# Charging a planner for VectorE's wait on GpSimd, moving weight sums between engines, and re-dividing PSUM banks

## Chip, cores and metric

The kernel runs on one core of one Trainium2 chip. The metric is device time in microseconds of one execution. The time before is 971.36 us, the median of three runs (970.76 to 972.66).

## What is computed

The reference chains three layers; every matrix product is done in float32 there, while the kernel uses pairs of float16 halves (a high and a low part) and three products in place of one.

```python
# attention: q, k, v are (4, 8, 576, 64), f is (4, 8, 576)
decay = cum[:, :, :, None] - cum[:, :, None, :]          # cum = cumsum(log f)
attn = softmax(where(causal, -1e9, q @ k.T / 8 + decay))
x = attn @ v                                             # -> 2304 tokens x 512
# first MLP: 512 -> 2048 -> 512
x = relu(x @ w_in) ** 2 @ w_out
# second MLP: 512 -> 1536 -> 512
out = (silu(x @ w_gate) * (x @ w_val)) @ w_out2
```

## The kernel before

**The order.** The kernel doesn't leave the order of its instructions to a scheduler. Each piece of work is a `Step` with an engine, an estimated duration, what it waits for, the buffers that it takes, and a priority; `Plan.order` plays the steps through in a model of the five engines and emits them in the order in which they started there. Each engine then runs its own list strictly in that order. The model has a rule for VectorE and GpSimd working at once: a step whose function name is in `SHARED` (for VectorE `lo`, `join`, `a2`, `v_lo`, `p_lo`; for GpSimd all its large ones) is lengthened by 0.95 (VectorE) or 0.45 (GpSimd) of its overlap with such a step of the other engine, and never by more than that share of its own duration. Priorities are numbers written out by hand: `EPRI` for the 16 first-half attention units, `VPRI` for the four batches of v, `IPRI`, `ILOAD`, `OPRI`, `OLOAD` for the first MLP's weights and their loads, `GPRI` for the second MLP's weights. A lower number goes first; evictions and the like have -100 to -120.

**The stages.** TensorE begins with 130 matmuls on constants (L295), the lowest priority of all, which the plan puts wherever TensorE would have nothing to do. First come the weights of the first MLP and the first 256 queries of each attention unit (half 0), then the first MLP's tiles `mlp1(j)`, interleaved with the other queries (half 1, tiles of up to 128 queries against up to 576 keys). `mlp1` goes over nine tiles of 256 tokens in the order 0, 1, 2, 3, 4, 5, 6, 8, 7. A tile is eight pairs: 24 matmuls up (L1152), relu and square on ScalarE (the square of the last two tiles on VectorE, `a2`, L1179), the high half on ScalarE (L1195), the low half on GpSimd (`g_lo`, L1198), and 24 matmuls down (L1220) into two PSUM accumulators, which are evicted to `tmp` buffers at the tile's end, one by ScalarE (L1239) and one by VectorE (L1241), and stored.

When attention has ended, its SBUF and PSUM are given to the second MLP. Its gate and value weights, in three chunks `u` each, need for each of the six chunks four sums of 128x512 elements, after Strassen and Winograd (`split7`: `tt`/`sum_of`, L507, all on GpSimd), before ScalarE and VectorE (L545) split seven blocks into halves. `tables2` (L1642 to L1649) works out three-column tables of scales on VectorE. `mlp2` then runs five rounds over two token tiles (one for the tail): the input's maximum (L1286, L1290), a matmul that spreads it over partitions (L1294), `scales` (L1298 to L1302, where L1300 and L1301 multiply three columns by one), four differences on GpSimd (L1317), seven splits (L1354 on ScalarE, `lo` L1358 on VectorE), and then six pairs of seven products (L1415), whose sums VectorE makes (L1432), silu and multiplication (L1456, L1460, L1464 `mul3`), and matmuls L1531 into four accumulators. Chunk `u` of the weights serves pairs 2u and 2u+1.

**PSUM.** Of eight banks `ps_acc` has 3 (accumulators of `mlp1`, and in the early stage the statistics of the first MLP's weights), `ps_h` 2, and `ps_at` (attention: scores take two, the product with v one) 3. In the second MLP `ps_at` becomes two `ps_v` banks and one `ps_l`, the fourth accumulator.

Of the kernel before, what the change touches and what calls it, by code (L numbers as in the profile page):

```python
# [57 lines left out]
class Plan:  # L58
# [9 lines left out]
    def add(self, eng, us, fn, deps=(), pri=0, take=(), use=(), nbytes=0, order=(), late=0.0):  # L68
        deps, order = ([d for d in ds if d is not None] for ds in (deps, order))
        st = Step(len(self.steps), eng, us, fn, deps, order, pri, take, nbytes)  # L70
        st.hot = getattr(fn, "__name__", "") in SHARED[eng] if eng in SHARED else False
        st.late = late
        for buf in (*take, *use):
            buf.users.append(st)
        self.steps.append(st)
        return st

    def order(self):
        now, dma_free = 0.0, 0.0
        free = {e: 0.0 for e in AFTER}  # L80
        hot = {DVE: 0.0, POOL: 0.0}
        landed = []
# [101 lines left out]
def decay_attention_moe_kernel(ctx: ExitStack, tc, q, k, v, f, w1, w2, wg, wv, wo, outT):  # L184
# [19 lines left out]
    HN = 2  # L204
    AN = 3
    XN = 2
# [11 lines left out]
    dpool = ctx.enter_context(tc.tile_pool(name="dram", bufs=1, space=bass.MemoryType.DRAM))  # L218
    ps_acc = ctx.enter_context(tc.tile_pool(name="ps_acc", bufs=3, space=bass.MemoryType.PSUM))
    ps_h = ctx.enter_context(tc.tile_pool(name="ps_h", bufs=HN, space=bass.MemoryType.PSUM))  # L220
# [92 lines left out]
    def bank(where):  # L313
        if where == "acc":
            return Buf("acc", 3), lambda: ps_acc.tile([P, 512], F32, tag="acc", name="ps")
# [169 lines left out]
    def split7(c, idx, slot, scaled):  # L485
# [18 lines left out]

        def tt(out, x, y, op):
# [8 lines left out]
        t2 = add(POOL, 0.3 + pool_us(512), tt(s2, s1, e0, ALU.subtract), [t1], pri, use=[r0])  # L514
        t3 = add(POOL, 0.3 + pool_us(512), tt(s3, e0, o0, ALU.subtract), [j0, j1], pri, use=[r0, r1])
        t4 = add(POOL, 0.3 + pool_us(512), tt(s4, e1, s2, ALU.subtract), [t2], pri, use=[r0, r1])

# [161 lines left out]
    def attn_unit(idx, b, pr, half, opened):  # L679
# [88 lines left out]
        for ti, i in enumerate(tiles):  # L768
# [14 lines left out]
            for h, r0, r1, qc, M, g in heads:  # L783
# [349 lines left out]
    def mlp_pair(t, j, p, np_, names, lag, xs, xbuf, xdeps):  # L1133
# [59 lines left out]
        def g_hi():  # L1193
            G[k0].append(mlp.tile([P, 2, 2, TN], F16, tag="g", bufs=GN, name="g"))
            nc.scalar.copy(G[k0][1][:, 0], G[k0][0])  # L1195

        def g_lo():
            nc.gpsimd.tensor_tensor(G[k0][1][:, 1], G[k0][0], G[k0][1][:, 0], op=ALU.subtract)  # L1198

        h = add(ACT, act_us(512) - 0.07, g_hi, [r], -100, take=[gb], use=[tmp])  # L1200
        l = add(POOL, pool_us(512), g_lo, [h], -100, use=[tmp, gb])
        nm = names[-1]
        if p == 0:
            A[t, j] = [None, None]
            ABUF[t, j] = [Buf("acc", 3), Buf("acc", 3)]
            STORED[t, j] = []
# [55 lines left out]
    def mlp2(n, js, gate):  # L1262
# [106 lines left out]
        if two:  # L1369
            accs = [Buf("acc", 3) for _ in range(3)] + [Buf("al", 1)]  # L1370
        else:
            accs = [Buf("acc", 3) for _ in range(2)]
        STORED[key] = []
# [5 lines left out]
        def acc_new(i):  # L1379
            shape = [P, 512] if two else [P, 2, TN]  # L1380
            if i == 3:
                acc[i] = pools["psl"].tile(shape, F32, tag="al", name="acc")
# [239 lines left out]
    def open_ex():  # L1622
# [5 lines left out]
        pools["psl"] = ctx.enter_context(  # L1628
            tc.tile_pool(name="ps_l", bufs=1, space=bass.MemoryType.PSUM, reuse_waits="tile")
        )  # L1630
# [90 lines left out]
```

## Time and profile before

| | |
|---|---|
| median of three runs | 971.36 us |
| the profiled execution's own time | 972.56 us |
| its span, first to last instruction | 970.9 us |
| TensorE matmul busy | 952.9 us, 98% of the span |
| VectorE, ScalarE, GpSimd busy | 629.4, 607.2, 352.3 us |

An engine's busy time is the union of its instructions' times. A wait of TensorE shows as idle time before an instruction, with the instruction on another engine that released it. The time outside the span (1.7 us) lies before the first and after the last instruction.

### The profile page before, as it was taken

The numbers are of one execution on the slowest core, as the hardware profiler recorded it, in microseconds if no ns is written. First come the engines' busy times: TensorE is split into PE (matmuls) and PEld (weight loads), VectorE is DVE, ScalarE is ACT, GpSimd is POOL, SyncE is SP. The second block draws the span as 40 slices with busy tenths as digits, with TensorE's granted clock in tenths as the row PEclk, the third lists the DMA queues.
The fourth block names the chain that finished last, engine by engine and source line by source line (L and its number), as shares of the span: only waits on it lengthen the run. The fifth ranks groups of instructions, "written<-read, shape, count | busy, mean of one in ns | idle before, by whom it ended". The sixth has DMA issues, their size and how long they took to land. (4 is left out here: it accounts for less than half of the span.)

```text
span 970.9 us, 22565 instructions
## 1 busy us (share of the span) xinstructions
PE 952.9 (98%) x8941; PEld 735.6 (76%) x8941; DVE 629.4 (65%) x1394; ACT 607.2 (63%) x1145; POOL 352.3 (36%) x440
## 2 busy tenths in 40 slices
PE   8999999999999999999999998999999999999998
PEld 3677777888777778777788887777978776877774
DVE  5778878576666687878799999345464363433341
ACT  5889898788777889867787766325443343332232
POOL 1322154354444544533285874122231231110120
PEclk8999999999999999999999999999999999999999
DMA  8697529676777879898943602002001001000101
GB/s 282 209 349 213 105 65 210 180 219 141 168 154 172 174 171 256 181 270 200 248 159 101 226 22 66 1 1 64 26 21 46 1 1 45 1 1 12 34 1 44
DMA packets 147945, 117.47 MB, mean 121 GB/s; under 512 B 98240, under 2 KB 136128, under 8 KB 142592
## 3 DMA queue, kind: packets, MB, share of 16 engines
q1 hardware_dynamic: 147840, 116.04, 45.8%
q8 instruction: 70, 1.15, 0.5%
q14 instruction: 35, 0.29, 0.1%
HBM read 83.44 MB, written 9.51 MB: 96 GB/s over the span
## 5 line engine op out<-in xcount | busy, mean ns | idle before, releaser
L1152 PE MATMUL h<-x,i 128*128 128x256 f16 x1728 | 210.5, 274 | 0.7 <-ACT hold L1174 0.7
L1220 PE MATMUL acc<-g,o 128*128 128x256 f16 x1728 | 208.0, 273 | 1.8 <-POOL g L1198 1.8
L1152 PEld LDWEIGHTS <-i 128*128 128x128 f16 x1728 | 163.1, 98 | 30.7 <-issue 9.6
L1220 PEld LDWEIGHTS <-o 128*128 128x128 f16 x1728 | 163.1, 98 | 29.6 <-issue 8.5
L1531 PE MATMUL acc<-o,f 128*128 128x512 f16 (+1 forms) x720 | 145.7, 358 | 0.5 <-ACT o L1504 0.5
L1531 PEld LDWEIGHTS <-f 128*128 128x128 f16 x720 | 69.9, 98 | 64.5 <-issue 0.8
L1198 POOL TENSOR_TENSOR g<-tmp,g 128x512 f16<-128x512 f32 x56 | 77.1, 1378 | 102.4 <-ACT g L1195 95.3
L1494 POOL TENSOR_TENSOR tmp<-tmp,o 128x256 f32<-128x256 f32 (+1 forms) x30 | 23.5, 784 | 246.9 <-ACT o L1488 246.9
L787 POOL TENSOR_SCALAR_AFFINE_SELECT bias<-bias 128x128 f32<-128x128 f32 (+1 forms) x160 | 68.0, 433 | 122.3 <-DVE cg L826 68.8
L846 ACT ACTIVATE s<-s,cg 128x256 f32<-128x256 f32 (+4 forms) x144 | 83.6, 582 | 21.4 <-DVE cg L826 21.0
L826 DVE CUSTOM_DVE_ANT_0 s<-ps,bias 128x512 f32<-128x512 f32 (+3 forms) x160 | 73.1, 481 | 32.6 <-PE ps L803 28.0
L909 DVE SCALAR_TENSOR_TENSOR p<-s,cg,p 128x512 f16<-128x512 f32 (+4 forms) x112 | 77.9, 710 | 25.2 <-ACT p L905 24.5
L905 ACT ACTIVATE p<-s,cg 128x512 f16<-128x512 f32 (+4 forms) x112 | 67.6, 619 | 13.0 <-DVE cg L859 4.0
L1415 PEld LDWEIGHTS <-g 128*128 128x128 f16 x720 | 65.4, 98 | 10.6 <-issue 2.7
L1460 ACT ACTIVATE r<-r,ms 128x768 f32<-128x768 f32 (+1 forms) x30 | 26.2, 872 | 73.9 <-DVE r L1432 73.7
L1415 PEld LDWEIGHTS <-v 128*128 128x128 f16 x720 | 65.4, 98 | 6.5
L1415 PE MATMUL v<-i,g 128*128 128x256 f16 (+1 forms) x540 | 67.9, 262 | 1.8 <-DVE r L1432 1.6
L1415 PE MATMUL v<-i,v 128*128 128x256 f16 (+1 forms) x540 | 67.9, 262 | 0.0
L1432 DVE TENSOR_TENSOR r<-r,h 128x512 f32<-128x512 f32 (+1 forms) x30 | 19.0, 633 | 72.6 <-PE h L1415 64.0
L1498 POOL TENSOR_TENSOR r<-r,o 128x768 f32<-128x768 f32 (+1 forms) x30 | 44.9, 1498 | 42.5 <-ACT o L1491 41.7
L1432 DVE TENSOR_TENSOR r<-r,v 128x512 f32<-128x512 f32 (+1 forms) x60 | 38.0, 633 | 34.1 <-PE v L1415 32.0
L1415 PEld LDWEIGHTS <-eg 128*128 128x128 f16 x540 | 49.3, 98 | 11.3 <-issue 2.5
(184 smaller groups left out, 1648.7 us busy)
## 6 DMA issues: line engine op xcount, KB each, us to landing
raw<-in_moe_w_out_dram SPq DMA_DIRECT2D x11, 1024.0 KB, 7.7
bias<-cum_d SPq DMA_DIRECT2D x16, 576.0 KB, 4.3
raw<-in_moe_w_val_dram SPq DMA_DIRECT2D x9, 1024.0 KB, 5.5
raw<-in_moe_w_gate_dram SPq DMA_DIRECT2D x9, 1024.0 KB, 7.0
raw<-in_moe_w_in_dram SPq DMA_DIRECT2D x8, 1024.0 KB, 6.7
vr<-in_v_dram SPq DMA_DIRECT2D x32, 256.0 KB, 4.1
x_d<-tmp SPq DMA_DIRECT2D x18, 256.0 KB, 2.8
kr<-in_k_dram SPq DMA_DIRECT2D x16, 288.0 KB, 4.1
```

The costliest lines, as they stand in the source:

```text
L787: nc.gpsimd.affine_select(diag, diag, pattern=[[-1, w]], compare_op=ALU.is_ge, fill=-8e9, base=0, channel_multiplier=1)
L826: nc.vector.tensor_tensor_reduce(out=s[r0:r1, n0:e1], in0=c["ps", ti, ci, h][r0:r1, : e1 - n0], in1=c["bias"][r0:r1, h, n0:e1], scale=-0.1 ...
L846: nc.scalar.activation(s[:, :ext], s[:, :ext], AF.Exp, bias=cg[:, mc : mc + 1], scale=-1.0, accum_out=cg[:, 2:3],)
L905: nc.scalar.activation(pv[:, 0, :ext], s[:, :ext], AF.Copy, scale=cg[:, 3:4])
L909: nc.vector.scalar_tensor_tensor(pv[:, 1, :ext], s[:, :ext], cg[:, 3:4], pv[:, 0, :ext], op0=ALU.mult, op1=ALU.subtract,)
L1152: nc.tensor.matmul(HP[key][:, u, :], w[:, wi, kk, c * P : (c + 1) * P], x[:, xi, kk, :], start=(kk == 0 and (wi, xi) == (0, 0)), stop=(kk ...
L1198: nc.gpsimd.tensor_tensor(G[k0][1][:, 1], G[k0][0], G[k0][1][:, 0], op=ALU.subtract)
L1220: nc.tensor.matmul(acc[:, d - part[0], :], w[:, wi, c, d * P : (d + 1) * P], G[k0][1][:, gi, u, :], start=(m == 0 and d == part[0] and (wi ...
L1415: nc.tensor.matmul(R[reg][:, which, :w], t[:, wh, w1_ : w1_ + P], x[:, xh, xi, kk], start=fresh and which == 0 and kk == 0 and (wh, xh) == ...
L1432: nc.vector.tensor_tensor(out(), x(), y(), op=ALU.add)
L1498: nc.gpsimd.tensor_tensor(g, g, R["g"][:, 0, 1:4], op=ALU.subtract)
L1531: nc.tensor.matmul(acc_of(d), wd[:, cc, d * P : (d + 1) * P], R["g"][:, gi, 2 * m : 2 * m + 2].rearrange("p a t -> p (a t)"), start=mm == ...
```

## The change

It alters five things. (1) The planner's rule for VectorE and GpSimd: every GpSimd step, and on VectorE the steps named in a shorter list with `mul3`, `g_lo` and `sum_of` added, now start late, by all (VectorE) or 0.45 (GpSimd) of what the other engine's step still has to run. (2) Three of the four sums of each weight chunk go to VectorE (`SUMV = 3`; the list `on` sends `t1`, `t2` and `t3` to VectorE and leaves `t4` on GpSimd). (3) `tables2` and `scales` multiply column by column, with a column as the scalar. (4) `ps_acc` gets two banks and `ps_at` four; the second MLP's accumulators are two of `ps_acc` and two of `ps_l`. (5) The hand-written priorities have other values. `GLO = 9` lets tiles from j = 9 on make the low half on VectorE; j ends at 8, so no tile does. The number of matmuls on constants stays 130.

```diff
+PORT = {DVE: 1.0, POOL: 0.45}
+GLO = 9
+SUMV = 3
-SHARED = {
-    DVE: ("lo", "join", "a2", "v_lo", "p_lo"),
-    POOL: ("sum_of", "diff_of", "g_lo", "gd1", "gd3", "k_lo", "q_lo", "mask"),
-}
-SLOW = {DVE: 0.95, POOL: 0.45}
+SHARED = ("lo", "join", "a2", "v_lo", "p_lo", "mul3", "g_lo", "sum_of")
...
-        st.hot = getattr(fn, "__name__", "") in SHARED[eng] if eng in SHARED else False
+        st.hot = eng == POOL or (eng == DVE and getattr(fn, "__name__", "") in SHARED)
...
-                    us = st.us
+                    begin = now
                     if st.hot:
-                        other = hot[POOL if e == DVE else DVE] - now
-                        us += SLOW[e] * max(0.0, min(us, other))
-                        hot[e] = now + us
-                    free[e] = now + us
-                    st.done = now + us + AFTER[e]
+                        begin += PORT[e] * max(0.0, port[POOL if e == DVE else DVE] - now)
+                        port[e] = begin + st.us
+                    free[e] = begin + st.us
+                    st.done = free[e] + AFTER[e]
...
-GPRI = 895
+GPRI = 863
...
-EPRI = [84, -11, -1228, -173, 17, 207, 26, -63, 272, 261, 415, 539, 152, 235, -12, -45]
-VPRI = [11, -292, 536, 601]
-IPRI, ILOAD = [303, -473, 276, 202], [-471, 170, 327, -259]
-OPRI, OLOAD = [279, 410, 340, 342], [-413, 225, 178, 605]
+EPRI = [97, 98, -1473, -437, 74, 58, -88, -342, 192, 243, 591, 593, 223, 341, 56, -118]
+VPRI = [79, -116, 547, 595]
+IPRI, ILOAD = [573, -458, 265, 171], [-574, -104, -303, 434]
+OPRI, OLOAD = [157, 400, 363, 178], [-547, 34, 61, 213]
...
-    AN = 3
+    AN, ACC = 4, 2
...
-                nc.gpsimd.tensor_tensor(out(), x(), y(), op=op)
+                (nc.vector if on[0] == DVE else nc.gpsimd).tensor_tensor(out(), x(), y(), op=op)
...
-        t1 = add(POOL, 0.3 + pool_us(512), tt(s1, o0, o1, ALU.add), [j0, j1], pri, use=[r0, r1])
...
+        on = [(DVE, dve_us(512)) if n < SUMV else (POOL, 0.3 + pool_us(512)) for n in (1, 2, 0, 3)]
+        t1 = add(*on[0], tt(s1, o0, o1, ALU.add, on[0]), [j0, j1], pri, use=[r0, r1])
...
-                masks.append(add(POOL, 0.42, mask, [lb, *before[h]], pri, use=[bias]))
+                masks.append(add(POOL, 0.3, mask, [lb, *before[h]], pri, use=[bias]))
...
-            nc.vector.tensor_scalar(ms[:, 10 : 10 + NG2], ISG, ms[:, 7:8], None, op0=ALU.mult)
-            nc.vector.tensor_scalar(ms[:, 16 : 16 + NG2], KV, ms[:, 8:9], None, op0=ALU.mult)
+            for u in range(NG2):
+                nc.vector.tensor_scalar(ms[:, 10 + u : 11 + u], ISG[:, u : u + 1], ms[:, 7:8], None, op0=ALU.mult)
+                nc.vector.tensor_scalar(ms[:, 16 + u : 17 + u], KV[:, u : u + 1], ms[:, 8:9], None, op0=ALU.mult)
...
-            accs = [Buf("acc", 3) for _ in range(3)] + [Buf("al", 1)]
+            accs = [Buf("acc", ACC) for _ in range(ACC)] + [Buf("al", 4 - ACC) for _ in range(4 - ACC)]
...
-        nc.vector.tensor_tensor(t[:, 0:NG2], ISG, ISV, op=ALU.mult)
+        for u in range(NG2):
+            times(t[:, u : u + 1], ISG[:, u : u + 1], ISV[:, u : u + 1])
...
-        nc.vector.tensor_tensor(KV, ISV, ISF, op=ALU.mult)
-        nc.vector.tensor_scalar(KV, KV, CC[:, 0:1], 2.0**-40, op0=ALU.mult, op1=ALU.mult)
+        for u in range(NG2):
+            times(KV[:, u : u + 1], ISV[:, u : u + 1], ISF[:, u : u + 1], CC[:, 0:1])
+            times(KV[:, u : u + 1], KV[:, u : u + 1], 2.0**-40)
```

## Rows read from the trace of the kernel before

**Rows 1.** The profile's page: busy us, share of the span, instructions of each engine

```profile
PE 952.9 (98%) x8941; PEld 735.6 (76%) x8941; DVE 629.4 (65%) x1394; ACT 607.2 (63%) x1145; POOL 352.3 (36%) x440
```

**Rows 2.** TensorE's waits: instruction, releaser; total us, times, longest us

```profile
PE v L1415 <- DVE r L1432: 2.5, 2, 1.6
PE acc L1220 <- POOL g L1198: 1.8, 1, 1.8
PE ps L1294 <- DVE sq L1290: 1.7, 1, 1.7
PE h L1415 <- DVE i L1358: 1.2, 1, 1.2
PE ps L326 <- DVE mt L1063: 1.1, 1, 1.1
PE ps L295 <- POOL ones L279: 1.1, 1, 1.1
PE ps L409 <- DVE raw L388: 1.1, 1, 1.1
PE ps L803 <- DVE x L984: 1.0, 1, 1.0
```

**Rows 3.** Windows: length, busy us (instructions) by engine, clock, DMA share, GB/s

```profile
20.00:40.00 20.00, 20.00 (x122) 11.78 (x121) 14.44 (x58) 16.85 (x38) 8.98 (x19) 0.85 0.75 223
...
480.00:605.00 125.00, 119.49 (x1122) 103.56 (x1121) 119.57 (x135) 92.27 (x119) 85.54 (x53) 1.00 0.37 122
605.00:971.00 366.00, 360.76 (x3000) 271.78 (x2997) 155.14 (x253) 128.76 (x225) 76.84 (x68) 1.00 0.06 20
```

**Rows 4.** The same window, the weight sums of L507 alone

```profile
480.00:605.00 125.00, 42.85 (x24) 1.00 0.37 122
```

**Rows 5.** VectorE's groups by shape, 480 to 605 us: busy us, mean ns

```profile
L1179 DVE SCALAR_TENSOR_TENSOR tmp<-tmp,al 128x512 f32<-128x512 f32 x16 | 21.6, 1355 | 1.8 <-ACT tmp L1174 1.8
...
L1301 DVE TENSOR_SCALAR ms<-kv,ms 128x3 f32<-128x3 f32 x2 | 2.9, 1428 | 0.0
L1432 DVE TENSOR_TENSOR r<-r,v 128x512 f32<-128x512 f32 x4 | 2.7, 676 | 0.0
...
L1300 DVE TENSOR_SCALAR ms<-swi,ms 128x3 f32<-128x3 f32 x2 | 1.9, 951 | 0.0
...
L1302 DVE TENSOR_SCALAR ms<-ms,cc 128x1 f32<-128x1 f32 x2 | 0.5, 261 | 0.0
...
L310 DVE TENSOR_SCALAR ms<-pw 128x1 f32<-128x1 f32 x2 | 0.3, 154 | 0.1
```

**Rows 6.** L1179 over the whole span: shortest, median and longest, in ns

```profile
L1179 DVE SCALAR_TENSOR_TENSOR tmp<-tmp,al x16: 736/1636/2065, 487.0 to 571.2; 128x512 f32<-128x512 f32 x16
```

**Rows 7.** VectorE in order of time: the tables' first and last instruction (of eight), then 551 to 556 us

```profile
518.82 1.11 DVE L1642 TENSOR_TENSOR t<-swi 128x3 f32<-128x3 f32 x1
...
524.14 0.14 DVE L1649 TENSOR_SCALAR cc<-cc 128x1 f32<-128x1 f32 x1
...
550.97 2.00 DVE L1179 SCALAR_TENSOR_TENSOR tmp<-tmp,al 128x512 f32<-128x512 f32 x1
...
555.20 0.50 DVE L1290 TENSOR_TENSOR sq<-ms 128x4 bf16<-128x4 f32 x1
```

**Rows 8.** GpSimd in order of time, at the same place

```profile
549.93 5.74 POOL L507 TENSOR_TENSOR raw<-raw 128x512 f32<-128x512 f32 x3 [1.16 <-DVE raw L388]
```

**Rows 9.** The chain that ended last: start, us, what (two pairs of the second MLP)

```profile
618.97 5.18 PE acc L1531 x24
...
633.32 5.18 PE acc L1531 x24
```

**Rows 10.** In order of time: a change of accumulators between two tiles

```profile
493.81 0.82 PE L1220 MATMUL acc<-g,o 128*128 128x256 f16 x6
...
494.75 0.69 ACT L1239 ACTIVATE tmp<-acc,fy 128x512 f32<-128x512 f32 x1 [0.91 <-DMA x_d<-tmp]
```

**Rows 11.** TensorE's matmuls on constants: count, busy us, mean ns

```profile
L295 PE MATMUL ps<-ones 128*128 128x512 bf16 x130 | 35.9, 416 | 1.3 <-POOL ones L279 1.1
```

More of the change, by code (lines that the diff above doesn't have):

```diff
@@ L80, in order @@
         free = {e: 0.0 for e in AFTER}
-        hot = {DVE: 0.0, POOL: 0.0}
+        port = {DVE: 0.0, POOL: 0.0}
         landed = []
@@ L218, in decay_attention_moe_kernel @@
     dpool = ctx.enter_context(tc.tile_pool(name="dram", bufs=1, space=bass.MemoryType.DRAM))
-    ps_acc = ctx.enter_context(tc.tile_pool(name="ps_acc", bufs=3, space=bass.MemoryType.PSUM))
+    ps_acc = ctx.enter_context(tc.tile_pool(name="ps_acc", bufs=ACC, space=bass.MemoryType.PSUM))
     ps_h = ctx.enter_context(tc.tile_pool(name="ps_h", bufs=HN, space=bass.MemoryType.PSUM))
@@ L314, in bank @@
         if where == "acc":
-            return Buf("acc", 3), lambda: ps_acc.tile([P, 512], F32, tag="acc", name="ps")
+            return Buf("acc", ACC), lambda: ps_acc.tile([P, 512], F32, tag="acc", name="ps")
         if where == "vp":
@@ L503, in part, with tt @@
             return piece["lo"].bitcast(F32).rearrange("p (b k a n) -> p b k a n", b=2, k=2, a=2)[:, n]
-        def tt(out, x, y, op):
+        def tt(out, x, y, op, on):
             def sum_of():
-                nc.gpsimd.tensor_tensor(out(), x(), y(), op=op)
+                (nc.vector if on[0] == DVE else nc.gpsimd).tensor_tensor(out(), x(), y(), op=op)
             return sum_of
@@ L512, in split7 @@
         s1, s2, s3, s4 = (lambda: part(p0, 0)), (lambda: part(p0, 1)), (lambda: part(p1, 0)), (lambda: part(p1, 1))
-        t1 = add(POOL, 0.3 + pool_us(512), tt(s1, o0, o1, ALU.add), [j0, j1], pri, use=[r0, r1])
-        t2 = add(POOL, 0.3 + pool_us(512), tt(s2, s1, e0, ALU.subtract), [t1], pri, use=[r0])
-        t3 = add(POOL, 0.3 + pool_us(512), tt(s3, e0, o0, ALU.subtract), [j0, j1], pri, use=[r0, r1])
-        t4 = add(POOL, 0.3 + pool_us(512), tt(s4, e1, s2, ALU.subtract), [t2], pri, use=[r0, r1])
+        on = [(DVE, dve_us(512)) if n < SUMV else (POOL, 0.3 + pool_us(512)) for n in (1, 2, 0, 3)]
+        t1 = add(*on[0], tt(s1, o0, o1, ALU.add, on[0]), [j0, j1], pri, use=[r0, r1])
+        t2 = add(*on[1], tt(s2, s1, e0, ALU.subtract, on[1]), [t1], pri, use=[r0])
+        t3 = add(*on[2], tt(s3, e0, o0, ALU.subtract, on[2]), [j0, j1], pri, use=[r0, r1])
+        t4 = add(*on[3], tt(s4, e1, s2, ALU.subtract, on[3]), [t2], pri, use=[r0, r1])
         def make(which):
@@ L1195, in g_hi @@
             nc.scalar.copy(G[k0][1][:, 0], G[k0][0])
+        lows = (DVE, dve_us(512), nc.vector) if j >= GLO else (POOL, pool_us(512), nc.gpsimd)
         def g_lo():
-            nc.gpsimd.tensor_tensor(G[k0][1][:, 1], G[k0][0], G[k0][1][:, 0], op=ALU.subtract)
+            lows[2].tensor_tensor(G[k0][1][:, 1], G[k0][0], G[k0][1][:, 0], op=ALU.subtract)
         h = add(ACT, act_us(512) - 0.07, g_hi, [r], -100, take=[gb], use=[tmp])
-        l = add(POOL, pool_us(512), g_lo, [h], -100, use=[tmp, gb])
+        l = add(lows[0], lows[1], g_lo, [h], -100, use=[tmp, gb])
         nm = names[-1]
@@ L1369, in mlp2 @@
         if two:
-            accs = [Buf("acc", 3) for _ in range(3)] + [Buf("al", 1)]
+            accs = [Buf("acc", ACC) for _ in range(ACC)] + [Buf("al", 4 - ACC) for _ in range(4 - ACC)]
         else:
-            accs = [Buf("acc", 3) for _ in range(2)]
+            accs = [Buf("acc", ACC) for _ in range(2)]
         STORED[key] = []
@@ L1380, in acc_new @@
             shape = [P, 512] if two else [P, 2, TN]
-            if i == 3:
+            if i >= ACC:
                 acc[i] = pools["psl"].tile(shape, F32, tag="al", name="acc")
@@ L1628, in open_ex @@
         pools["psl"] = ctx.enter_context(
-            tc.tile_pool(name="ps_l", bufs=1, space=bass.MemoryType.PSUM, reuse_waits="tile")
+            tc.tile_pool(name="ps_l", bufs=4 - ACC, space=bass.MemoryType.PSUM, reuse_waits="tile")
         )
@@ L1641, in tables2, with times @@
         t = small.tile([P, NG2 + 1], F32, tag="t2", bufs=1, name="t2")
-        nc.vector.tensor_tensor(t[:, 0:NG2], ISG, ISV, op=ALU.mult)
+        def times(out, x, y, z=None):
+            nc.vector.tensor_scalar(out, x, y, z, op0=ALU.mult, **({} if z is None else {"op1": ALU.mult}))
+        for u in range(NG2):
+            times(t[:, u : u + 1], ISG[:, u : u + 1], ISV[:, u : u + 1])
         nc.vector.tensor_reduce(CC[:, 2:3], t[:, 0:NG2], axis=mybir.AxisListType.X, op=ALU.max)
         nc.vector.tensor_reduce(CC[:, 3:4], ISF, axis=mybir.AxisListType.X, op=ALU.max)
-        nc.vector.tensor_tensor(CC[:, 3:4], CC[:, 3:4], CC[:, 2:3], op=ALU.mult)
+        times(CC[:, 3:4], CC[:, 3:4], CC[:, 2:3])
         nc.vector.reciprocal(CC[:, 0:1], CC[:, 3:4])
-        nc.vector.tensor_tensor(KV, ISV, ISF, op=ALU.mult)
-        nc.vector.tensor_scalar(KV, KV, CC[:, 0:1], 2.0**-40, op0=ALU.mult, op1=ALU.mult)
-        nc.vector.tensor_scalar(CC[:, 3:4], CC[:, 3:4], 2.0**40, None, op0=ALU.mult)
-    tab2[0] = add(DVE, 1.6, tables2, [*SCALES["f"], *SCALES["g"], *SCALES["v"]], GPRI)
+        for u in range(NG2):
+            times(KV[:, u : u + 1], ISV[:, u : u + 1], ISF[:, u : u + 1], CC[:, 0:1])
+            times(KV[:, u : u + 1], KV[:, u : u + 1], 2.0**-40)
+        times(CC[:, 3:4], CC[:, 3:4], 2.0**40)
+    tab2[0] = add(DVE, 2.3, tables2, [*SCALES["f"], *SCALES["g"], *SCALES["v"]], GPRI)
     for j in (2, 3, 4, 5, 6, 8, 7):
```

2 lines of the change are left out of this document (1 added, 1 removed).

## The prediction

> **What bounds the kernel now.** I read the page first. TensorE is busy 952.9 of 970.9 us [rows 1]; the other engines are far from full over the whole span. The difference, 18.0 us, is all that any change of order can bring as long as TensorE's own work stays the same, and the change touches no matmul: products, shapes and the 130 matmuls on constants [rows 11] are as before. These last fill early idle time, so they show as busy; if the plan finds less idle time early, they only stand elsewhere.
>
> Next I read TensorE's waits, for what the 18.0 us are made of. The eight longest add up to 11.5 us [rows 2]; the rest is small waits and the drain after the last matmul. Of the 11.5, 8.6 are waits for VectorE, 2.9 for GpSimd.
>
> Then the windows, to see where. From 480 to 605 us TensorE is idle for 5.5 us, and there VectorE is busy for 119.57 of 125 us; from 605 us on it is busy for 155 of 366 [rows 3]. The waits for L1432, L1290 and L1358 (2.5, 1.7, 1.2; 5.4 us) [rows 2] belong to that crowded stretch, where the second MLP's weights are prepared beside the last tiles of the first.
>
> Last the shapes within it. L1179, one operation of one size, takes 0.736 us at its shortest and 1.355 us on average [rows 5, 6]: 0.62 us, sixteen times 9.9 us, in which VectorE is held up. The order of time shows by whom: L1290, four columns, ends 555.70, just after GpSimd's sum, which ends 555.67 [rows 7, 8]; L1179 before it takes 2.00 us beside the same sums. So a VectorE operation of this kind waits until GpSimd's running one has ended.
>
> **The column products.** L1300 and L1301, three columns, take 0.95 and 1.43 us on average in the crowded stretch; a single column takes 0.154 (L310) or 0.27 us (L1302) there [rows 5], with GpSimd as busy as ever. Two rounds' `scales` fall in the stretch: 2 x (0.95 + 1.43) = 4.76 us become twelve columns, 1.8 to 3.2 us; 1.6 to 2.9 us less. `tables2` takes from 518.82 to 524.28, 5.46 us [rows 7]; fourteen instructions at 0.154 to 0.27 make 2.2 to 3.8; 1.7 to 3.3 us less. I take 2.3 and 2.5. The later three rounds have VectorE time to spare [rows 3], so what they gain or lose there costs nothing.
>
> **The sums.** Eighteen of 24 leave GpSimd. All 24 take 42.85 us there [rows 4], so its 85.54 us in the stretch fall by 32.1 to 53.4, from 68% to 43% of it. VectorE's price isn't in the trace. Below stands L1432, the same shape with one operand in PSUM, 0.676 us; above L1179, the same shape, held up, 1.355 us [rows 5]: 12.2 to 24.4 us. With GpSimd less busy a sum would lose 0.62 x 43/68 = 0.39 us, and cost 1.07; I take that, nearer the middle: 19.2 us. What VectorE gets back: L1179's losses fall from 9.9 to 6.2 us, 3.7 less, and as an estimate as much again for the other splits and joins; 7.4 us. With the columns' 4.8 us VectorE's account is +19.2 - 12.2 = +7.0 us, or 0.0 with sums at the lower price. It has 5.4 us idle in the stretch, and the third weight chunk isn't wanted before the round's fifth pair; a pair takes 14.35 us [rows 9], so what is added can lie behind 605 us, where VectorE is under half busy. That is the cover. If the plan doesn't use it, up to 7 us come out at TensorE. The sums issue no DMAs, and behind them in VectorE's list stand splits of the same weights; a step that TensorE waits for stands behind one sum at most if the plan lets it go ahead.
>
> Taking GpSimd's sums out of the way frees the two chains that TensorE waited for: at 551 to 556 us L1179 and L1290 would have cost 0.74 and about 0.15 in place of 2.00 and 0.50, 1.6 of the 1.7 us; in the first round's start 0.8 to 1.5 of the 1.2 us are the columns'. Late next would be the splits L1358 behind GpSimd's differences, which stay. I take half of the 5.4 us: **-2.7** (ends: -5.4, and +7.0 as above).
>
> On this the Trainium skill speaks against the change: its page SBUF — State Buffer, section "Who interferes with whom", says that a VectorE instruction with two SBUF inputs contends with a GpSimd one that reads SBUF, and that whichever comes second is blocked for the whole instruction, either way. L1290 [rows 7] agrees for VectorE. By that rule all eighteen sums are exposed, and the planner's 0.45 for GpSimd is too little; its result is the first rival below.
>
> **The planner's rule and the new order.** It changes where everything stands and so can end or make any wait. I price it by the waits outside the stretch. L326's wait for L1063 (1.1 us, the statistics of weights read ahead) [rows 2]: half, **-0.5**. TensorE's wait for GpSimd's low half (L1198, 1.8) [rows 2]: half, **-0.9** (ends -1.8 and 0). The starts (L295, L409; 1.1 each) I leave. Between 20 and 40 us the clock was 0.85 of full [rows 3], partly at the lower of its two levels (1.2 of 2.4 GHz): 20 x 0.15 = 3 us, which followed TensorE's early waits. Other early priorities can save it or cost it again: 0, ends -3 and +3.
>
> **The banks.** A fourth attention bank lets the next scores start while a product is drained: the wait for L984 (1.0) goes, **-1.0**. Attention may also end earlier and give the crowded stretch more room; I count nothing for it. A third accumulator less: at the change of tiles shown, the next tile's first matmul ran at 493.81, while the old bank was evicted until 495.44 [rows 10], 1.6 us later. TensorE has upward matmuls to put in between, so I take **+1.0** for all eight changes (ends 0 and 8 x 1.6 = 13). In the second MLP there are four accumulators before and after: 0. The mask's smaller price in the plan, and `GLO`, move no work: 0.
>
> **Sum.** -2.7 - 0.5 - 0.9 - 1.0 + 1.0 = -4.1. The profiled execution took 972.56 us, its span 970.9; it becomes 968.5. The median of the runs lies 1.2 us under the profiled one, so the forecast for it is 971.36 - 4.1 = 967.3 us.
>
> **Rivals.** *VectorE too full.* In the crowded stretch the sums cost what I took or more, and the plan sets them ahead of what TensorE needs. For it: 119.57 of 125 us busy. Against: room after 605 us. It decides from the point where a sum costs over some 1.0 us with nothing put off: then 12.2 us of relief are used up and 5.4 us of idle time begin to go. At +7 less the 2.4 us of the other terms without the accumulators': 971.4 + 4.6 = 976 us.
>
> *Accumulators.* With two banks each of eight changes waits for both evictions; at half of the 1.6 us each, in place of the +1.0: 971.4 - 5.1 + 6.4 = 972.7; at the whole, 979. Against: the second bank's eviction already stood between tiles before.
>
> *Waits only change places.* A new order has its own few microseconds of mishaps, as this one has; 11.5 us of named waits stay 11.5: 971.4 us.
>
> *All of it.* The waits for VectorE outside the starts (7.5 us: 5.4, 1.1, 1.0), GpSimd's 1.8 and the 3 us of clock go, with no cost from the accumulators: 971.4 - 12.3 = 959.1; with VectorE's waits alone, 963.9.
>
> **How the numbers follow.** The forecast has 0.42 (own range 964 to 969.4), all of it 0.15, change of places 0.22, VectorE too full 0.13, accumulators 0.08. 0.2% of 971.36 is 1.9 us, about what a measurement of this kernel can tell from no change. Faster: 0.42 + 0.15 = 0.57; the same: 0.22; slower: 0.13 + 0.08 = 0.21. The range goes from just under the lowest case, 959, to VectorE too full, 976, and leaves out the accumulators' far end.
>
> **What would show it.** In the trace after, L1300, L1301 and `tables2` as single columns at 0.15 to 0.27 us beside a busy GpSimd; sums on VectorE between 0.68 and 1.36 us; L1179's mean well under 1.355; GpSimd near 53 us between 480 and 605; the waits for L1290, L1358 and L1432 together under 3 us; no wait of scores for a bank; no new wait of L1220 for L1239 or L1241. The prediction is wrong if TensorE's idle time isn't near 14 us, if its busy time moves by more than 2 us, or if the early clock is lost for longer.

## The result, and the profile after

The changed kernel takes 957.73 us (median of four runs, 957.51 to 958.73), the one before 971.42 beside it: a ratio of 0.986, with an interval of 0.9842 to 0.9877. It gains 13.7 us where the forecast had 4.1, and it ends just below the range. Of the rivals, *All of it* (959.1 us) comes nearest.

The page of the profile after, engine by engine as in [rows 1] (the profiled execution took 958.73 us):

```profile
span 957.0 us, 22589 instructions
...
PE 945.6 (99%) x8941; PEld 735.7 (77%) x8941; DVE 621.3 (65%) x1438; ACT 603.4 (63%) x1145; POOL 315.2 (33%) x422
```

TensorE's idle time falls from 18.0 to 11.4 us. But its busy time falls as well, from 952.9 to 945.6 us for the same 8941 matmuls. The forecast had the busy time unchanged.

TensorE's waits, which answer to [rows 2]; these are the longest now:

```profile
PE ps L407 <- DVE raw L386: 1.1, 2, 0.6
PE ps L293 <- POOL ones L277: 1.1, 1, 1.1
PE ps L802 <- DVE cg L825: 0.9, 1, 0.9
PE h L1151 <- ACT hold L1173: 0.7, 1, 0.7
PE ps L955 <- DVE cg L825: 0.5, 1, 0.5
...
PE ps L324 <- DVE mt L415: 0.4, 1, 0.4
PE acc L1533 <- DVE tmp L1564: 0.4, 1, 0.4
```

Lines have moved by one to five (L1415 is now L1417, L1220 is L1221, L507 is L505). The two waits at the start, for `raw` and for `ones`, are still there. The 5.4 us for L1432, L1290 and L1358, the 1.8 us for GpSimd's low half, the 1.1 us for L1063 and the 1.0 us for L984 have gone. The first MLP (L1221) waits for no accumulator's eviction, but the second does once, for 0.4 us at 710.9 us: L1564 evicts an accumulator. The 0.9 us for L825, also an operation that reads an attention bank, stand at 30.6 us, far from L984's place (424.9 us), and four other traces of the same order (a_order_only, a_sums_gpsimd, a_sum2, a_cols3) don't have them; the 0.5 us of L955 they all have.

The same windows as in [rows 3]:

```profile
20.00:40.00 20.00, 19.01 (x108) 10.57 (x107) 12.81 (x59) 16.18 (x41) 8.29 (x21) 0.91 0.80 268
480.00:605.00 125.00, 125.00 (x1131) 108.88 (x1129) 105.66 (x156) 86.10 (x114) 52.56 (x35) 1.00 0.31 102
605.00:971.00 366.00, 346.27 (x2880) 260.19 (x2878) 149.67 (x256) 124.24 (x218) 75.54 (x66) 1.00 0.06 20
```

In the crowded stretch TensorE is busy for all of 125 us. GpSimd has 52.56 us in place of 85.54, as forecast. VectorE, which was to get 7 us more or the same, has 13.9 us less. Part of that is work that the new order does earlier: over the whole span VectorE is busy for 8.1 us less (629.4 to 621.3).

VectorE's groups by shape in that stretch, which answer to [rows 5] (busy us, mean ns of one):

```profile
L1178 DVE SCALAR_TENSOR_TENSOR tmp<-tmp,al 128x512 f32<-128x512 f32 x15 | 12.7, 857 | 3.3 <-ACT tmp L1173 3.3
...
L505 DVE TENSOR_TENSOR raw<-raw 128x512 f32<-128x512 f32 x10 | 7.4, 781 | 0.0
...
L1303 DVE TENSOR_SCALAR ms<-kv,ms 128x1 f32<-128x1 f32 x6 | 1.3, 209 | 0.0
...
L1302 DVE TENSOR_SCALAR ms<-swi,ms 128x1 f32<-128x1 f32 x6 | 1.2, 202 | 0.0
...
L1646 DVE TENSOR_SCALAR kv<-swi,cc 128x1 f32<-128x1 f32 x3 | 0.8, 269 | 0.0
```

The ten sums of L505 in this list take 0.78 us on average, and five more have other operands. The same stretch with the sums of L505 alone, VectorE's first and then GpSimd's:

```profile
480.00:605.00 125.00, 10.66 (x15) 11.43 (x5) 1.00 0.31 102
```

So VectorE is busy for 0.71 us for each of its fifteen sums, close to the lower bound of 0.676, not the 1.07 taken. L1178 (L1179 before) falls from 1.355 to 0.857 us. Single columns take 0.20 to 0.27 us, as forecast.

Two more places of TensorE in order of time. The first shows a change that no forecast term covers, the second answers to [rows 10]:

```profile
339.92 1.06 PE L802 MATMUL ps<-KA,Q 64*64 64x288 f32 x12
...
486.20 3.45 PE L1221 MATMUL acc<-g,o 128*128 128x256 f16 x30
```

Twelve score matmuls stand in one run here, and before they came in runs of six, with upward matmuls in between. Counted in the trace, leaving out the matmuls on constants, the places where TensorE passes from work on attention or statistics to MLP work or back are 313 before and 285 after. The places where it passes between matmuls on 64 rows or 64 columns of the array and all others are 286 and 258. Either way 28 go. (An expectation below has 414 and 381; the traces don't bear these out.) The start of the first downward matmul of the first MLP's tile 7 (493.81 us before) is at 486.20.

With that start and the start of the 841st product of the second MLP (L1415, now L1417) as marks, the time divides like this (us, from the traces; the rows with a label are experiments told of below):

| kernel | to tile 7 | tile 7 to product 841 | from there to the last matmul |
|---|---|---|---|
| before | 493.8 | 193.3 | 279.0 |
| after's order, all sums on GpSimd, three columns (a_order_only) | 483.5 | 194.0 | 279.6 |
| after's order, all sums on GpSimd (a_sums_gpsimd) | 484.5 | 193.5 | 279.6 |
| after's order, two of four sums on VectorE (a_sum2) | 485.4 | 187.8 | 279.6 |
| after | 486.2 | 186.2 | 279.6 |
| after's order, all sums on VectorE (a_sum4) | 487.2 | 186.8 | 279.6 |
| before's order, three of four sums on VectorE (b_sums_vector) | 491.9 | 191.9 | 279.0 |

Half of the gain, 7.6 us, stands ahead of 486 us. Eight of the 24 sums have started there, the first at 470.8 us (four before the same mark in the kernel before), but from then on to the mark TensorE waits for nothing, and with all sums on GpSimd it comes no later. The other half, 7.1 us, stands in the crowded stretch; the last part is 0.6 us longer. One trace isn't sharp ahead of tile 7: the rows of after's order differ there by 3.7 us, in part by the clock from 20 to 40 us (0.91 to 1.00), and b_cols below, in before's order, is there at 490.8.

### The profile page after: what moved, and what is told of

The parts are those of the page before. It is cut to its first block, busy times and chain, and to the rows that moved or that the text cites. A ratio compares the mean times of both kernels' runs of the same rounds, so it can differ in the third digit from the quotient of the medians.

```text
span 957.0 us, 22589 instructions
## 1 busy us (share of the span) xinstructions
PE 945.6 (99%) x8941; PEld 735.7 (77%) x8941; DVE 621.3 (65%) x1438; ACT 603.4 (63%) x1145; POOL 315.2 (33%) x422
## 4 chain that ended last, share of the span: by engine, by line
PE 54%; DVE 1%; ACT 0%; issue 0%; DMA 0%; SPq 0%; DVEq 0%; ACTq 0%
PE v L1417 15%; PE acc L1533 14%; PE h L1417 11%; PE acc L1221 7%; PE h L1151 6%; PE ps L955 1%; PE ps L802 1%; DVE ms L1287 0%; DVE p L908 0%; DVE s L825 0%; DMA out_dram<-tmp 0%; DVE sq L1291 0%; SPq L1591 0%; DVE VT L630 0%; DVE tmp L1564 0%
## 5 line engine op out<-in xcount | busy, mean ns | idle before, releaser
L1151 PE MATMUL h<-x,i 128*128 128x256 f16 x1728 | 208.4, 273 | 0.7 <-ACT hold L1173 0.7
L1221 PE MATMUL acc<-g,o 128*128 128x256 f16 x1728 | 208.0, 273 | 0.0
L1221 PEld LDWEIGHTS <-o 128*128 128x128 f16 x1728 | 163.8, 98 | 27.4 <-issue 6.0
L1199 POOL TENSOR_TENSOR g<-tmp,g 128x512 f16<-128x512 f32 x56 | 76.1, 1360 | 130.7 <-ACT g L1194 126.0
L786 POOL TENSOR_SCALAR_AFFINE_SELECT bias<-bias 128x128 f32<-128x128 f32 (+1 forms) x160 | 60.9, 390 | 106.3 <-DVE cg L825 58.3
L825 DVE CUSTOM_DVE_ANT_0 s<-ps,bias 128x512 f32<-128x512 f32 (+3 forms) x160 | 72.6, 481 | 29.4 <-PE ps L802 21.4
L1417 PEld LDWEIGHTS <-g 128*128 128x128 f16 x720 | 65.4, 98 | 8.5 <-issue 0.6
L1417 PEld LDWEIGHTS <-v 128*128 128x128 f16 x720 | 65.4, 98 | 6.5
L1417 PE MATMUL v<-i,g 128*128 128x256 f16 (+1 forms) x540 | 67.9, 262 | 0.2 <-DVE tmp L1434 0.2
L1417 PE MATMUL v<-i,v 128*128 128x256 f16 (+1 forms) x540 | 67.9, 262 | 0.0
L1417 PEld LDWEIGHTS <-eg 128*128 128x128 f16 x540 | 49.3, 98 | 8.9
```

Of the source, the lines that this page charges most:

```text
L786: nc.gpsimd.affine_select(diag, diag, pattern=[[-1, w]], compare_op=ALU.is_ge, fill=-8e9, base=0, channel_multiplier=1)
L825: nc.vector.tensor_tensor_reduce(out=s[r0:r1, n0:e1], in0=c["ps", ti, ci, h][r0:r1, : e1 - n0], in1=c["bias"][r0:r1, h, n0:e1], scale=-0.1 ...
L1151: nc.tensor.matmul(HP[key][:, u, :], w[:, wi, kk, c * P : (c + 1) * P], x[:, xi, kk, :], start=(kk == 0 and (wi, xi) == (0, 0)), stop=(kk ...
L1199: lows[2].tensor_tensor(G[k0][1][:, 1], G[k0][0], G[k0][1][:, 0], op=ALU.subtract)
L1221: nc.tensor.matmul(acc[:, d - part[0], :], w[:, wi, c, d * P : (d + 1) * P], G[k0][1][:, gi, u, :], start=(m == 0 and d == part[0] and (wi ...
L1417: nc.tensor.matmul(R[reg][:, which, :w], t[:, wh, w1_ : w1_ + P], x[:, xh, xi, kk], start=fresh and which == 0 and kk == 0 and (wh, xh) == ...
```

## The experiments

Two theories. **Sums**: what pays is GpSimd's time, because its low halves (L1199), which TensorE waits for, and the users of the sums no longer come late. **Order and banks** (the rival): what pays is the new order of TensorE's work, which the planner's rule, the priorities and the banks make together, whoever adds the weights.

### Parts of the change, with the order held

These five keep the order of every engine as it was and change only where or in what form an instruction runs.

**a_sums_gpsimd** (after; all 24 sums on GpSimd)

```
-                (nc.vector if on[0] == DVE else nc.gpsimd).tensor_tensor(out(), x(), y(), op=op)
+                nc.gpsimd.tensor_tensor(out(), x(), y(), op=op)
```

> The changed kernel with its instructions in the very same order, but all 24 weight sums issued on GpSimd at the places where 18 of them stood on VectorE. Theory 1, the engines' load is what the stretch from 480 to 605 us gained by: GpSimd is busy there for about 85 us again, VectorE's splits wait for it, and most of the 7 us that the stretch gained come back as waits of TensorE for L1434, L1360 and L1291: 963 to 966 us. Theory 2, the order is what gained: the sums are off TensorE's path, 958 to 960 us.

Measured: 963.94 us beside 970.49, a ratio of 0.9934 (0.9917 to 0.9952). About half of the gain is lost, and the table shows where: all of it after tile 7. Its waits, and the crowded stretch:

```profile
PE acc L1221 <- ACT tmp L1240: 2.4, 1, 2.4
PE acc L1221 <- ACT g L1194: 1.3, 1, 1.3
...
PE acc L1221 <- POOL g L1199: 1.0, 1, 1.0
```

```profile
480.00:605.00 125.00, 120.23 (x1069) 103.57 (x1067) 104.92 (x136) 85.72 (x112) 74.67 (x49) 0.99 0.30 102
```

GpSimd in order of time (start, us; in brackets the idle time ahead of an instruction and what ended it):

```profile
505.76 8.64 POOL L505 TENSOR_TENSOR raw<-raw 128x512 f32<-128x512 f32 x4
514.37 1.60 POOL L1199 TENSOR_TENSOR g<-tmp,g 128x512 f16<-128x512 f32 x1
...
525.31 4.27 POOL L505 TENSOR_TENSOR raw<-raw 128x512 f32<-128x512 f32 x2
...
539.04 6.19 POOL L505 TENSOR_TENSOR raw<-raw 128x512 f32<-128x512 f32 x3
547.06 2.27 POOL L1199 TENSOR_TENSOR g<-tmp,g 128x512 f16<-128x512 f32 x2 [1.84 <-ACT g L1194]
```

And the same place in the kernel after:

```profile
505.45 1.41 POOL L1199 TENSOR_TENSOR g<-tmp,g 128x512 f16<-128x512 f32 x1 [2.65 <-ACT g L1194]
509.96 3.61 POOL L505 TENSOR_TENSOR raw<-raw 128x512 f32<-128x512 f32 x1 [3.10 <-DVE raw L505]
513.53 1.61 POOL L1199 TENSOR_TENSOR g<-tmp,g 128x512 f16<-128x512 f32 x1
517.50 2.06 POOL L1199 TENSOR_TENSOR g<-tmp,g 128x512 f16<-128x512 f32 x1 [2.37 <-ACT g L1194]
```

With all sums on it GpSimd works for 8.64 us without a break, and the low half starts at once behind them: it was due earlier. In the kernel after, GpSimd mostly stands idle ahead of a low half and waits for ScalarE. The longest wait, 2.40 us until 529.01, comes by another road, which ScalarE in order of time shows:

```profile
527.18 1.21 ACT L541 ACTIVATE eg<-raw,sws 128x1024 f16<-128x1024 f32 x1 [1.00 <-POOL raw L505]
528.30 0.67 ACT L1240 ACTIVATE tmp<-acc,fy 128x512 f32<-128x512 f32 x1
```

L541 takes a sum as input and waits for GpSimd; behind it in ScalarE's list stands the eviction L1240 of one of the two accumulators, and TensorE needs that bank. Whether a third accumulator would have hidden this, no run shows. The three waits make 4.7 us; only the road of the longest was followed back. The other two end at 547.0 and 548.3 us, and right behind them TensorE's clock falls. Over ten microseconds it is 0.83 of full where the kernel after has 1.00, so partly at the lower level of 1.2 GHz; that is another 1.7 us:

```profile
545.00:555.00 10.00, 7.73 (x56) 6.00 (x55) 5.86 (x12) 4.91 (x7) 4.73 (x5) 0.83 0.33 107
```

VectorE, on the other hand, is busy for 104.92 us here and for 105.66 us with fifteen of the sums added: on VectorE they came out nearly free.

**a_cols3** (after; `scales` and `tables2` with the three-column instructions of before) and **b_cols** (before; with the single columns)

```
-            for u in range(NG2):
-                nc.vector.tensor_scalar(ms[:, 10 + u : 11 + u], ISG[:, u : u + 1], ms[:, 7:8], None, op0=ALU.mult)
...
+            nc.vector.tensor_scalar(ms[:, 10 : 10 + NG2], ISG, ms[:, 7:8], None, op0=ALU.mult)
```

> The changed kernel in the very same order, with the tables and the scales as three-column instructions again. Theory 1: each of the scales' two instructions waits for a GpSimd operation in the first two rounds, up to 1.2 us each, on TensorE's path at the round's start: 1 to 3 us slower, 959 to 961 us. Theory 2: the order leaves room before the splits, and nothing changes: 957.5 to 958.5 us.

> The kernel before in its own order, with tables and scales column by column and nothing else. Theory 1: the scales of the first two rounds take 0.8 to 1.5 us less each, on the path of the waits for L1358 and L1432: 1.5 to 2.5 us faster, 969 to 970 us. Theory 2: the waits only move to what stands next in VectorE's list: within 0.5 us of before.

Measured: a_cols3 959.52 us beside 970.49, 0.9888 (0.9871 to 0.9906), up to 0.3% behind the kernel after, with the two intervals overlapping; b_cols 969.85, 1.0 (0.9984 to 1.0015), nothing. In before's order VectorE's 119.57 us in the stretch become 116.38, so the columns gave 3.2 of the 4.8 us forecast, and TensorE got nothing of it:

```profile
480.00:605.00 125.00, 120.06 (x1099) 103.58 (x1097) 116.38 (x148) 90.56 (x116) 87.00 (x52) 1.00 0.35 117
```

In a_cols3, in the same stretch, three columns take 0.36 and 0.78 us, where they took 0.95 and 1.43 beside the busier GpSimd of before [rows 5]:

```profile
L1302 DVE TENSOR_SCALAR ms<-kv,ms 128x3 f32<-128x3 f32 x2 | 1.6, 778 | 0.0
L1301 DVE TENSOR_SCALAR ms<-swi,ms 128x3 f32<-128x3 f32 x2 | 0.7, 356 | 0.0
```

So once the sums are off GpSimd, a round's six single columns (1.23 us) cost VectorE in the stretch about what two instructions of three cost (1.13). In the three later rounds three columns take 0.21 and 0.23 us in either kernel, and six single ones cost 0.8 us more. The columns are a remedy for a hold-up that the sums already end in large part.

**b_sums_vector** (before; three of four sums on VectorE, in before's order)

```
-        def tt(out, x, y, op):
+        def tt(out, x, y, op, eng=nc.vector):
             def sum_of():
-                nc.gpsimd.tensor_tensor(out(), x(), y(), op=op)
+                eng.tensor_tensor(out(), x(), y(), op=op)
...
-        t4 = add(POOL, 0.3 + pool_us(512), tt(s4, e1, s2, ALU.subtract), [t2], pri, use=[r0, r1])
+        t4 = add(POOL, 0.3 + pool_us(512), tt(s4, e1, s2, ALU.subtract, nc.gpsimd), [t2], pri, use=[r0, r1])
```

> The kernel before in its own order, with three of four weight sums issued on VectorE at the places that they had on GpSimd. Theory 1: GpSimd's busy time in 480 to 605 us falls by 32 us and VectorE is held up less; the 5.4 us of waits there are halved or more, 966 to 969 us. Theory 2: VectorE gets 12 to 19 us more in a stretch with 5.4 us to spare, in an order that wasn't made for it: slower, 972 to 978 us.

Measured: 969.45 us beside 970.49, 0.9981 (0.997 to 0.9992). GpSimd falls to 52.67 us in the stretch, just as in the kernel after, and yet only 1 to 2 us come of it:

```profile
PE acc L1220 <- POOL g L1198: 1.6, 1, 1.6
PE ps L335 <- DVE top L332: 1.6, 1, 1.6
PE v L1415 <- DVE r L1432: 1.4, 1, 1.4
PE ps L326 <- DVE mt L1063: 1.4, 1, 1.4
...
PE ps L326 <- DVE mt L417: 1.0, 1, 1.0
```

L1198 (at 125 us) and L1063 (at 471 us) lie ahead of the first sum and have nothing to do with the sums. In the stretch the wait for L1290 has gone, those for L1358 and L1432 have shrunk, from 3.7 us to 1.6. But two new ones have come, together 2.5 us, for L332 and L417, which stand right behind sums in VectorE's list (at 497 to 501 us). Both theories are right in part: the sums end waits and make others. Moving them is worth 1 to 2 us in the old order and about 6 in the new one.

**a_order_only** (after's order; sums on GpSimd and three columns: both edits above together)

> The changed kernel in the very same order, with all 24 sums on GpSimd and the three-column instructions: what is left of the change is its order (rule and priorities) and its banks. Theory sum of parts: 6.2 us for the sums and 1.8 for the columns come on top of 957.7, 965 to 967 us, and order with banks is worth some 5 us against before. Theory fit: the order only works with the sums on VectorE, 969 to 973 us, and nothing is left.

Measured: 963.47 us beside 971.9, 0.9917 (0.99 to 0.9934). The order and the banks alone bring about 8 us, more than half of the gain. That is the rival's share, and it lies ahead of tile 7.

### How many sums, and what a change of work costs

**a_sum2** and **a_sum4** (after's order; two, and all four, of four sums on VectorE)

```
-                (nc.vector if on[0] == DVE else nc.gpsimd).tensor_tensor(out(), x(), y(), op=op)
+                eng.tensor_tensor(out(), x(), y(), op=op)
...
-        t3 = add(*on[2], tt(s3, e0, o0, ALU.subtract, on[2]), [j0, j1], pri, use=[r0, r1])
+        t3 = add(*on[2], tt(s3, e0, o0, ALU.subtract, on[2], nc.gpsimd), [j0, j1], pri, use=[r0, r1])
```

(a_sum2, where `t4` gets the same and `eng` is VectorE otherwise; in a_sum4 every sum is issued as `nc.vector.tensor_tensor`.)

> The kernel after in its own order, with two of four Strassen sums on VectorE and two on GpSimd. All four on GpSimd cost 6.2 us beside the kernel after. If the cost goes evenly with the count of sums on GpSimd, this is a third of that: 959.5 to 960.5. If what counts is that GpSimd is not yet late by the time of its next low half (rival), two on GpSimd still fit and the time is that of the kernel after within 1 us.

> The kernel after in its own order, with the fourth Strassen sum on VectorE too (24 of 24). If taking sums off GpSimd is what pays, by its 5.3 us of GpSimd time for each, a fourth on VectorE is a little faster or equal (955.5 to 958); if VectorE is near its limit in the stretch (108.9 of 125 us busy, rival), the six more sums of about 1 us each bring a wait back (960 to 964).

Measured: a_sum2 958.85 us beside 971.15, 0.9874 (0.985 to 0.9898); a_sum4 959.06, 0.988 (0.9858 to 0.9902). Both equal the kernel after within their intervals. So the first theory's even price per sum falls, and the threshold stands: two of four on GpSimd still fit in, with 1.2 us of idle time of TensorE in the stretch, and four of four don't. That VectorE is near its limit falls too: in a_sum4 TensorE is idle for 0.45 us of the stretch, by this wait for an eviction on VectorE:

```profile
PE acc L1221 <- DVE tmp L1242: 0.5, 1, 0.5
```

The engines' busy time over the whole span, in a_sums_gpsimd (no sum on VectorE), a_sum2 (12) and a_sum4 (24):

```profile
PE 947.9 (99%) x8941; PEld 736.2 (77%) x8941; DVE 622.8 (65%) x1420; ACT 604.6 (63%) x1145; POOL 341.6 (35%) x440
```

```profile
PE 944.6 (99%) x8941; PEld 735.0 (77%) x8941; DVE 622.4 (65%) x1432; ACT 603.7 (63%) x1145; POOL 321.6 (34%) x428
```

```profile
PE 944.5 (99%) x8941; PEld 735.2 (77%) x8941; DVE 621.8 (65%) x1444; ACT 602.1 (63%) x1145; POOL 303.5 (32%) x416
```

VectorE's total is the same with 0, 12, 18 (621.3) and 24 sums. What a sum costs it, it gets back in hold-ups that end.

**t_changes** (after, with a block of junk matmuls behind the last product, to price a change between full-array matmuls and those that use 64 rows or 64 columns of the array)

```
...
+        for _ in range(2):
+            for other, n in ((score, 6), (product, 12)):
+                for k in range(8 * REP):
+                    dense(k)
+                for k in range(n * REP):
+                    other(k)
+                for _ in range(REP):
+                    for k in range(8):
+                        dense(k)
+                    for k in range(n):
+                        other(k)
```

> The kernel after, with a block of TensorE work behind its last product, twice over: 240 full-array matmuls (128 rows, 256 columns) and 180 score-like ones (64 rows, 288 columns, fp32r) first apart and then mixed (8 and 6 in turn, 30 times, 60 changes of kind), and the same with 360 products into 64 of the array's columns (12 in turn). The output is unchanged, the time means nothing; the length of each part is read from the trace. If a change of kind costs what the steps between neighbours in the kernel suggest (93 to 124 ns), the mixed part takes 5.6 to 7.4 us longer than the apart one. If changes of kind are free (rival), and the busy time fell for another reason, mixed and apart agree within 1 us.

Measured in the second round, windows with TensorE's busy time: scores apart, scores mixed, products apart, products mixed.

```profile
1116.99:1155.34 38.35, 38.35 (x424) 1.00 0.01 1
1155.34:1202.53 47.19, 47.19 (x422) 1.00 0.00 1
1202.53:1239.01 36.48, 36.48 (x603) 1.00 0.01 2
1239.01:1281.95 42.94, 42.94 (x604) 1.00 0.01 2
```

The mixed parts issue the same matmuls, at the same clock, with no wait, and take 8.84 and 6.46 us longer for 58 more changes: 152 ns for a change to and from scores, 111 ns for products. All of it shows as busy time. The first round agrees within 0.2 us. (The scores are fp32r beside bf16, so there the type changes as well; the products are bf16 like the rest.) So 28 changes fewer are worth 3.1 to 4.3 us. That a change costs something is shown; that these 28 bring just this in the kernel is worked out from it.

### The planner's parts, each alone

These are planned anew, so every engine's order differs from both kernels. Each takes one part of the change out or puts one in.

**b_banks42** (before, planned with two accumulators and four attention banks), **b_newrule** (before, with the new rule for VectorE and GpSimd), **b_newpri** (before, with the new priorities), **a_oldrule** (after, with the old rule). Their edits are the like parts of the change, forward or back.

> The kernel before, planned anew with two accumulator banks and four attention banks, nothing else. Theory banks: with the fourth bank score groups stand next to each other, TensorE changes between attention and the MLP less often than the 414 times of before (381 in the changed kernel, at about 0.1 us each), and the wait of scores for L984 goes: 966 to 968 us. Theory priorities: without priorities made for it the order has as many mishaps as before: 969 to 974 us, changes near 414.

> The kernel before, planned anew with the changed planner's rule (late starts in place of longer steps, the new list), nothing else. Theory rule: steps that TensorE waits for are put ahead of GpSimd's sums, and the waits for VectorE in 480 to 605 us, 5.4 us, fall by half: 966 to 969 us. Theory priorities: another order with other mishaps, 969 to 974 us.

> The kernel before, planned anew with the changed priorities, nothing else. Theory priorities: most of the 7.5 us that the sums don't explain are in the order of loads and attention units: 963 to 967 us. Theory fit: the priorities only serve the plan that they came with (four attention banks, sums on VectorE), and here they are just another order: 969 to 976 us.

> The changed kernel, planned anew with the rule of before; sums, columns, banks and priorities stay changed. Theory rule: an order made without VectorE's real waits puts steps where VectorE isn't free: 961 to 965 us, new waits for VectorE or GpSimd in 480 to 605 us. Theory load: sums and columns have taken the contention away, so the rule has little left to say: 957 to 959.5 us.

Measured, each beside 970.06 us: 984.12, 1.0137 (1.0114 to 1.016); 997.26, 1.0275 (1.0252 to 1.0298); 985.92, 1.0158 (1.0134 to 1.0182); 1004.45, 1.0348 (1.0326 to 1.037). Every part put in or taken out alone makes the kernel slower. In b_banks42 the changes between attention and the MLP do fall, to 285 as in the kernel after, so the banks are enough for that (the rule alone brings 293, the priorities alone 299). But its busy time, 953.9 us, shows no saving as it stands: the clock was 0.91 from 20 to 40 us and 0.96 from 480 to 605, and new waits outweigh the rest. Two of the four show the kind of mishap. With the banks alone, at the turn to the second MLP:

```profile
PE h L1415 <- ACT r L1442: 9.7, 1, 9.7
PE acc L1220 <- POOL g L1198: 4.0, 2, 2.5
```

With the old rule, at the very start, where statistics of weights come too late:

```profile
PE ps L328 <- DVE mt L419: 25.0, 2, 16.2
PE ps L328 <- DVE pw L307: 8.4, 3, 7.1
```

**a_gpri873** and **b_gpri905** (one priority, `GPRI`, put up by 10 in either kernel, the rest untouched), to see what a plan that nobody has fitted costs

> The changed kernel planned anew with one number altered a little: the priority of the second MLP's weights 873 in place of 863. Nothing that the change speaks of is different. Theory fit: the order falls apart as with the other new plans, 965 to 985 us. Theory smooth: within 2 us of the changed kernel, 956 to 960 us.

> The kernel before planned anew with the same priority at 905 in place of 895. Theory fit: 975 to 990 us, as for its other new plans. Theory smooth: within 2 us of before, 968 to 973 us.

Measured beside 971.9 us: 966.44, 0.9942 (0.9924 to 0.9961), and 978.55, 1.0073 (1.0055 to 1.009). A step of 10 in one priority costs 0.7 to 0.8% in both. Both kernels thus stand at a fitted point, as far as one step each can tell, and a replanned experiment can carry 7 to 8 us of misfit that has nothing to do with the part tried. The 14 to 34 us above are more than that, but what each part is worth can't be read from them.

**a_sumv0** (after, planned anew with `SUMV = 0`: the plan knows that all sums are on GpSimd)

> The changed kernel planned anew with all sums on GpSimd. Theory load: the plan finds room for them, and the loss is that of the same order with sums on GpSimd or less, 960 to 964 us. Theory fit: priorities fit one plan alone, and any other is worse whatever its merit: above 968 us.

Measured: 961.43 us beside 971.9, 0.9898 (0.9881 to 0.9915). Where the plan can make room for GpSimd's sums, the kernel is 3.7 us slower than the kernel after, not six; as this one is replanned too, that is no clean price of the sums.

No version beat the kernel after. Three accumulators with the new priorities, and before's priorities under the new rule with the new banks, were not tried; how the 8 us of the order divide between rule, priorities and banks stays open.

## Why the prediction was wrong

**The ceiling.** "The difference, 18.0 us, is all that any change of order can bring as long as TensorE's own work stays the same" is the first step that failed: it takes the same products and shapes for the same busy time, and so puts a change of it at nothing. The matmuls do stay the same, but they are busy for 7.3 us less, where the prediction itself names 2 us as a sign of being wrong. Two things make up nearly all of it. The 28 fewer changes of work are worth 3.1 to 4.3 us, by t_changes. The other is the granted clock of the two profiled executions: before had 0.98 from 0 to 20 us, 0.85 from 20 to 40 [rows 3] and 0.91 from 420 to 440, the kernel after 0.91 from 20 to 40 and 1.00 in the other two. That is 3.4 us more lost before. From 420 to 440 us, before and then after:

```profile
420.00:440.00 20.00, 18.88 (x195) 13.86 (x194) 15.29 (x44) 14.69 (x33) 7.76 (x13) 0.91 0.92 235
420.00:440.00 20.00, 19.95 (x241) 16.00 (x234) 16.76 (x47) 17.12 (x36) 9.50 (x15) 1.00 1.01 262
```

The forecast had the clock at 0, with ends of 3 us either way. This part belongs to the execution and not to the order: b_cols and b_sums_vector, in before's order, had 0.92 and 0.93 from 20 to 40 us and 1.00 from 420 to 440, much like the kernel after, and were busy for 950.6 and 950.5 us. By these, 4.9 us of busy time are the order's, against 3.1 to 4.3 by the count of changes; the difference, 0.6 to 1.8 us, stays open. By idle time alone the gain would have been 6.6 us.

**The crowded stretch.** The mechanism was right: with GpSimd's sums gone, VectorE's waits there end. The term was mis-sized. I halved the 5.4 us to -2.7 because VectorE's account came out at +7.0; measured, all 5.4 go, TensorE has no idle time left in the stretch, and the part from tile 7 to product 841 is 7.1 us shorter. The account failed at the price of a sum, 0.71 us in place of 1.07, and above all at what VectorE gets back: in the same order fifteen sums add 0.7 us to it. The Trainium skill's rule (SBUF — State Buffer, "Who interferes with whom"), by which every one of the sums is exposed, doesn't show as a loss in VectorE's total here: of the fifteen in the stretch one was held up (1.65 us), and the others took 0.67 to 0.70. It is nearer the truth for GpSimd, whose five remaining sums in the stretch take 1.50 to 3.61 us, 2.3 on average, against 1.79 before [rows 4].

I also named the wrong chain. I took VectorE's hold-ups as what the sums cost. In the new order the sums on GpSimd cost 6 us by GpSimd's own lateness, at its low halves and at what ScalarE makes of the sums, and by the clock that fell behind these waits, and VectorE is as busy with them as without.

**The rule and the order.** -0.5 and -0.9 were half of two waits; both waits go whole, 2.9 us. Order and banks alone bring 8 us (a_order_only), by fewer changes as well, and that part isn't in any wait.

**The banks.** +1.0 for the accumulators was 0 in the first MLP: no eviction is waited for there. In the second MLP, priced at 0, it was 0.4 us, the wait for L1564; b_banks42, with two accumulators and before's priorities, has it too. -1.0 for the fourth attention bank came, at L984, but the products' 0.5 us for L825 stand against it. What two and four banks let the plan do, fewer changes of work (285 with the banks alone), I had priced at nothing.

**The columns.** Their cost was right (0.20 to 0.27 us each). Their worth at TensorE is 0 in before's order and at most 0.3% in after's.

**The rivals.** *VectorE too full* fell with a_sum4: 24 sums, and 0.5 us of waiting in the stretch. *Accumulators* fell for this plan, but it isn't idle: with the sums on GpSimd L1221 waits 2.4 us for the eviction L1240, and in a_sum4 0.5 us for L1242. *Waits only change places* is what b_sums_vector and the replanned kernels do. *All of it* had the right waits, and left out the changes of work and the new small waits; that it comes within 1.4 us of the result is in part luck.

## What to carry to other kernels

A busy engine isn't full of work that must be: count how often a bound TensorE changes between kinds of matmul before calling its idle time the ceiling. When an edit comes with a new order, hold the order and undo the edit, and also keep the edit's order alone; here the two halves, the sums and the order, were of about equal size, and only the first stood in the profile's waits. An order fitted by search is a point, not a part: one priority moved by 10 cost 0.7 to 0.8%, so a part tried in a replanned kernel tells little.

## What the runs showed of the hardware that was not expected

- A change between full-array matmuls and ones on 64 columns cost TensorE 111 ns of busy time, one to and from ones on 64 rows (and from bf16 to fp32r) 152 ns, with no wait and the clock at 1.00 (t_changes).
- VectorE's busy time was 622.8, 622.4, 621.3 and 621.8 us with 0, 12, 18 and 24 additions of 128x512 moved to it from GpSimd: each cost it about 0.7 to 0.8 us and freed it of as much.
- An instruction of three columns took 0.95 to 1.43 us beside a GpSimd busy for 68% of the time, 0.36 to 0.78 beside one busy for 42%, and 0.21 to 0.23 in the later rounds.
